# The last chunk's fourth column group: 120 rows in a load of their own, 8 rows beside the tokens, with products of their own

## The chip, the cores and the metric

The kernel runs on one core of one Trainium2 chip. The metric is the device time of one execution in microseconds, the median of several runs. The engines are TensorE (PE, with its weight loads as PEld), VectorE (DVE), ScalarE (ACT), GpSimd (POOL) and SyncE (SP). Loads and stores are issued by SP and ACT and carried out by 16 DMA engines.

## The reference

One decode step for a batch of 8 tokens, all in float32: layernorm, attention over a window of 1024 cached positions, a residual, a second layernorm, a gated MLP and a second residual.

```python
W = min(4096, max(256, Sk // 4))                 # Sk = 4096: W = 1024
q = (x @ wq) ...                                 # x: 8 x 1024, 32 heads of 128
scores = jnp.einsum("bhqd,bhkd->bhqk", q, k) * (Dh ** -0.5)   # the last W positions
p = _softmax(scores, axis=-1)
o = jnp.einsum("bhqk,bhkd->bhqd", p, v) ...  @ wo
...
g = jnp.einsum("bsd,df->bsf", x, w_gate)         # w_gate, w_up: 1024 x 3584
u = jnp.einsum("bsd,df->bsf", x, w_up)
h = _gelu(g) * u
return jnp.einsum("bsf,fd->bsd", h, w_down)      # w_down: 3584 x 1024
...
x = A_x
h = x + _A_ref(_layernorm(x, axis=-1), A_k_cache, A_v_cache, A_wq, A_wo)
h2 = h + _B_ref(_layernorm(h, axis=-1), B_w_gate, B_w_up, B_w_down)
```

## The kernel before

The weights and the caches are 111 MB and are read once. The host lays them out so that each load fills whole rows of SBUF: 128 partitions, each with one contiguous row in HBM. Two buffers, `buf[0]` and `buf[1]`, of 64 KB in each partition are filled in turn. SP issues the loads in the order of use, each with a wait for the products that last read the part of the buffer that it fills, and the queue is nearly always full.

TensorE runs one loop of seven passes: pass 0 is the query projection, 1 the scores, 2 the values, 3 the output projection, 4 (`GU0`) and 5 (`GU1`) gate and up, 6 (`DN`) down. In a pass, `products(0)` works on buffer 0 (gate, in passes 4 and 5) and `products(1)` on buffer 1 (up). A product has 32 columns of weights (8 tokens, 4 times), so it fills one of four column groups of the array, and four products that write partitions 0-31, 32-63, 64-95 and 96-127 of PSUM run beside each other. A float32 product is two matmuls in the trace. Ahead of each step TensorE waits for the semaphore `go`. GpSimd gives it: for each step it waits for all that the step needs and then counts `go` up. `turn` transposes activations (eight transposes of 128 x 128). Repeated products of no use (`repeat_residual`, L470) stand in two places of the loop.

The 3584 features of the MLP are 28 chunks of 128. `at` holds them transposed, 32 columns for a chunk. The down projection takes most chunks in the loop (pass 6, loads `wd0` to `wd2`, with 5, 2 and 1 of the 8 steps). Chunks 24 to 26 come after the loop in three loads of 128 rows by 4 KB, `ws0` to `ws2`. The last chunk, 27 (`LAST`), is cut by columns into four groups of 256 (`QW`), one for each column group, and loaded in two halves, `we0` and `we1`, with 128 of the 256 columns of each group (`ENDS`); a row of such a half is 2 KB.

After the loop TensorE does, in this order: the products of `ws0` (L534, into `ob[0]`), of `ws1` (L527, into `fin`), the fold of the sums of the loop, `d1` (L527, with `add2`), the products of `ws2` (L527), of `we0` and of `we1` (L551, into `ob[1]`). VectorE makes `d1` (L412, L415). ScalarE copies `fin` to `s_sb` (L417) once the products of `ws2` are done. VectorE adds `ob[1]` to it, one half after `we0` and one after `we1` (L421), and the two halves of the result are stored, `out0` from SP and `out1` from ACT.

The tokens `x` (8 rows of 4 KB) are loaded at the start from ACT's queue into partitions 0, 8, ..., 56 of `x_sb`, which GpSimd clears ahead of that (L177); every other partition of `x_sb` stays zero.

## Time and profile before

| | us |
|---|---|
| median of 3 runs | 264.74 (264.09 to 265.97) |
| the profiled execution: time | 264.55 |
| its span in the trace | 263.1 |
| PE busy | 149.2 |
| ACT busy | 31.1 |
| DVE busy | 26.8 |
| q1 (SP's loads), share of 16 DMA engines over the span | 98.4% |

The difference between time and span, 1.45 us, lies around the execution and is not in the trace. Busy time of an engine is a sum over the span; what sets the end is read from the chain of work that ended last.

### The profile page before, as it was taken

How to read it: one execution, taken by the hardware profiler on the slowest of the kernel's cores; microseconds unless marked ns; L12 is line 12 of the kernel's file. 1: busy time of each engine (PE TensorE's matmuls, PEld its weight loads, DVE VectorE, ACT ScalarE, POOL GpSimd, SP SyncE). 2: the span in 40 equal slices, each digit the busy share in tenths (PEclk: the TensorE clock that was granted, in tenths of full speed). 3: DMA queues.
4: the chain of work that ended last, by engine and by line, in shares of the span. 5: the costliest groups of instructions: out<-in, count | busy, mean ns of one | idle time of the engine just before them, and what ended most of it. 6: DMA issues, size and time to landing. Idle time of an engine off the chain costs nothing. (4 is left out here: it accounts for less than half of the span.)

```text
span 263.1 us, 2355 instructions
## 1 busy us (share of the span) xinstructions
PE 149.2 (57%) x1012; PEld 49.4 (19%) x1012; DVE 26.8 (10%) x45; ACT 31.1 (12%) x51; POOL 5.8 (2%) x12
## 2 busy tenths in 40 slices
PE   0024915916716717727518708817909509997985
PEld 0021211211111112122102202203302202322221
DVE  0400000000100100310500100250000200102011
ACT  1030110130020020010010000043200200201100
POOL 8000000000000000000000000000000000000000
PEclk9999985895975975956965965975976956999999
DMA  7999997999799799979979997999899999999995
GB/s 299 423 418 458 478 478 319 478 478 468 329 478 478 329 468 478 468 329 478 478 339 458 478 468 329 478 478 448 349 404 468 404 473 404 443 467 405 396 408 214
DMA packets 3617, 111.32 MB, mean 423 GB/s; under 512 B 408, under 2 KB 664, under 8 KB 1312
## 3 DMA queue, kind: packets, MB, share of 16 engines
q1 hardware_dynamic: 3456, 111.22, 98.4%
q10 hardware_dynamic: 160, 0.10, 0.1%
q14 instruction: 1, 0.01, 0.0%
HBM read 111.18 MB, written 0.13 MB: 423 GB/s over the span
## 5 line engine op out<-in xcount | busy, mean ns | idle before, releaser
L484 PE MATMUL o<-w,st 128*32 128x512 f32 x832 | 115.8, 716 | 73.7 <-PEq L457 66.9
L484 PEld LDWEIGHTS o<-w,st 128*32 128x32 f32 x832 | 32.0, 129 | 149.9 <-issue 149.9
L464 PE MATMUL tt<-ident,zeros 128*128 128x128 f32 x104 | 16.5, 311 | 35.1 <-PEq L457 35.1
L464 PEld LDWEIGHTS tt<-ident,zeros 128*128 128x128 f32 x104 | 13.3, 159 | 45.5 <-issue 45.5
L470 PE MATMUL fin<-zeros,spread 128*32 128x512 f32 x24 | 10.6, 593 | 0.0
L330 ACT COPY st<-tt 128x512 f32<-128x512 f32 x4 | 2.1, 588 | 36.2 <-PE tt L464 36.2
L320 DVE SCALAR_TENSOR_TENSOR av<-o,rtot,own 128x512 f32<-128x512 f32 x4 | 3.0, 752 | 31.3 <-PE o L484 31.3
L305 ACT ACTIVATE zeros<-o,nmax 128x1024 f32<-128x1024 f32 x2 | 2.2, 1113 | 31.9 <-DVE nmax L303 31.9
L303 DVE TENSOR_REDUCE nmax<-o 128x1 f32<-128x1024 f32 x2 | 2.4, 1224 | 34.7 <-PE o L484 34.7
L345 DVE TENSOR_TENSOR y_sb<-o,y_sb 128x512 f32<-128x512 f32 x3 | 2.1, 690 | 35.8 <-PE o L484 35.8
L285 DVE SCALAR_TENSOR_TENSOR zeros<-o,tq 128x512 f32<-128x512 f32 x2 | 1.4, 690 | 38.1 <-PE o L484 38.1
L379 DVE TENSOR_TENSOR g<-o,g 128x512 f32<-128x512 f32 x2 | 1.4, 691 | 30.6 <-PE o L484 30.6
L388 DVE TENSOR_TENSOR u<-o,u 128x512 f32<-128x512 f32 x2 | 1.4, 692 | 28.4 <-PE o L484 28.4
L284 ACT ACTIVATE tq<-o 128x512 f32<-128x512 f32 x2 | 1.2, 597 | 24.9 <-PE o L484 24.9
L470 PEld LDWEIGHTS fin<-zeros,spread 128*32 128x32 f32 x24 | 2.6, 110 | 7.2 <-issue 7.2
L352 ACT COPY zeros<-fin 32x512 f32<-32x512 f32 x1 | 0.6, 574 | 28.1 <-PE fin L515 28.1
L323 DVE TENSOR_REDUCE zeros<-av 128x128 f32<-128x1024 f32 x2 | 3.7, 1872 | 0.1
L214 POOL MEMSET zeros<- 128x3712 f32 x1 | 3.2, 3191 | 0.0
L378 ACT COPY g<-o 128x512 f32<-128x512 f32 x2 | 1.2, 585 | 16.8 <-PE o L484 16.8
L268 ACT COPY st<-tt 128x1024 f32<-128x1024 f32 x2 | 2.0, 1012 | 7.6 <-PE tt L464 7.6
L252 ACT ACT_TABLE_LOAD x2 | 2.6, 1283 | 2.9 <-POOL ident L211 2.9
L387 ACT COPY u<-o 128x512 f32<-128x512 f32 x2 | 1.2, 585 | 13.6 <-PE o L484 13.6
(58 smaller groups left out, 41.2 us busy)
## 6 DMA issues: line engine op xcount, KB each, us to landing
w<-ends SPq DMA_DIRECT2D x4, 4096.0 KB, 23.4
w<-w SPq DMA_DIRECT2D x1, 7168.0 KB, 21.8
w<-ends SPq DMA_DIRECT2D x1, 5120.0 KB, 21.6
w<-ends SPq DMA_DIRECT2D x1, 2048.0 KB, 26.1
w<-ends SPq DMA_DIRECT2D x3, 512.0 KB, 17.8
w<-w SPq DMA_DIRECT2D x1, 1024.0 KB, 4.9
w<-ends SPq DMA_DIRECT2D x1, 1024.0 KB, 28.1
w<-ends SPq DMA_DIRECT2D x2, 256.0 KB, 18.9
```

The source lines that it names most:

```text
L214: clear = run("gpsimd", lambda e: e.memset(zeros, 0.0))
L252: tok = run("scalar", lambda e: e.activation(sd, ve, AF.Sqrt), tok)
L268: a = run("scalar", lambda e: e.copy(st[0].rearrange("p (c r b) -> p c r b", c=NC, b=B), xt.unsqueeze(2).to_broadcast([P, NC, P // B, B])) ...
L303: tok = run("vector", lambda e: e.tensor_reduce(out=nmax, in_=ob[s], axis=AX.X, op=ALU.max, negate=True), pe(f"{h}1"))
L305: tok = run("scalar", lambda e: e.activation(xs[s], ob[s], AF.Exp, bias=nmax, accum_out=tot), tok)
L320: tok = run("vector", lambda e: e.scalar_tensor_tensor(av[:, i], o3, rtot, own.unsqueeze(2).to_broadcast([P, HB, DH]), op0=ALU.mult, op1=A ...
L323: tok = run("vector", lambda e: e.tensor_reduce(out=out, in_=av.rearrange("p i b d -> p d (i b)"), axis=AX.X, op=ALU.add), tok)
L330: tok = run("scalar", lambda e: e.copy(heads[:, g], turned.unsqueeze(2).to_broadcast([P, REP, P // 2 // B, B])), pe(f"t{h}2"))
L345: tok = run("vector", lambda e: e.tensor_add(y_sb, part, y_sb), ready, tok)
L464: ins = nc.tensor.transpose(t8[:, i, :], src[:, i * P:(i + 1) * P], ident)
L470: nc.tensor.matmul(fin[0:32, 0:N], spread.rearrange("p r b -> p (r b)"), h_sb[:, 0:N], start=True, stop=True)
L484: ins = nc.tensor.matmul(ob[s][32 * r:32 * r + 32, c:c + N], st[s][:, i * P + 32 * r:i * P + 32 * r + 32], buf[s][:, (i * NQ + r) * N:(i * ...
```

## The change

Of the last chunk's fourth column group (128 rows by 256 columns, 1 KB a row), the first 120 rows (`FEW`) are loaded by a load of their own, `w4`, into 120 partitions. The other 8 rows are appended to the tokens: each of the 8 rows of `x` becomes 5 KB, and `xw` takes the place of `x_sb`. `we0` and `we1` lose that group, so that their rows are 1.5 KB, and their products go from four to three each.

The fourth group is then two products into partitions 96-127 of `fin` (`ROW3` on), ahead of those of `ws0`: `at_odd` by `w_odd` (the 8 rows, on the 64 partitions of `xw`), and the first 120 partitions of `at` for chunk 27 by `w4`. The first of them starts the sum there, so the products of `ws1` no longer start it in that group. `at_odd` holds the 8 features of the 8 rows in partitions 0, 8, ..., 56. For that GpSimd clears 64 columns of `xs[1]` and writes the product of `ge` and `u1` for the last 8 features to every eighth of them; the transposes of pass 5 turn them with the rest, and ScalarE copies them out. The step of those transposes (`tb5`) waits for GpSimd's product too.

At the end ScalarE copies `fin` to `o_fin` itself, and VectorE adds into 96 of its partitions in place. The count of `gate` moves from ACT to SP.

```diff
+FEW = P - P // 16
+ROW3 = 32 * (NQ - 1)
...
-    x_sb = sb("x_sb", ROWS, D)
-    x_zero = run("gpsimd", lambda e: e.memset(x_sb, 0.0))
+    xw = sb("xw", ROWS, D + QW)
+    x_sb, w_odd = xw[:, 0:D], xw[:, D:]
+    x_zero = run("gpsimd", lambda e: e.memset(xw, 0.0))
...
-    x_in = move("x", x_sb[0:ROWS:STEP, :], x, x_zero, engine="scalar")
+    x_in = move("x", xw[0:ROWS:STEP, :], x, x_zero, engine="scalar")
...
+    t = buf[1][0:FEW, SINGLE * D:SINGLE * D + QW]
+    fourth = t, move("w4", t, fourth, pe(f"b{GU1}"))
     singles = []
...
-        a = SINGLE * D + NQ * c0
-        t = buf[1][:, a:a + NQ * n]
+        a = SINGLE * D + QW + (NQ - 1) * c0
+        t = buf[1][:, a:a + (NQ - 1) * n]
...
             late_ok = widen(STEPS // 2, STEPS, at_ok)
+            h0 = 32 * (nb - 1)
+            at_odd = sb("at_odd", ROWS, 32)
+            at_ok = run("scalar", lambda e: e.copy(at_odd, t8[0:ROWS, NC // 2, h0:h0 + 32]), pe(f"tb{k}"))
...
-    s_sb = sb("s_sb", P, QW)
-    sum_ok = run("scalar", lambda e: e.copy(s_sb, fin[:, 0:QW]), (fl.own["tensor"], len(names) + 2))
     o_fin = sb("o_fin", P, QW)
+    sum_ok = run("scalar", lambda e: e.copy(o_fin, fin[:, 0:QW]), (fl.own["tensor"], len(names) + 2))
     cut = ENDS[0]
-    halves = [(ob[1][:, 0:cut], 0, cut), (ob[1][:, N:N + QW - cut], cut, QW)]
-    done = [run("vector", lambda e: e.tensor_add(o_fin[:, a:b], d_ps, s_sb[:, a:b]),
+    halves = [(ob[1][0:ROW3, 0:cut], 0, cut), (ob[1][0:ROW3, N:N + QW - cut], cut, QW)]
+    done = [run("vector", lambda e: e.tensor_add(o_fin[0:ROW3, a:b], d_ps, o_fin[0:ROW3, a:b]),
...
-    nc.scalar.sem_inc(gate, 1)
     nc.vector.wait_ge(gate, 1).then_inc(gate, -1)
-    nc.sync.wait_ge(issued, 1)
+    nc.sync.wait_ge(issued, 1).then_inc(gate, 1)
...
+    odd = xs[1][:, N:N + ROWS]
     for name in [n for kind, n in order if kind == "wait"]:
+        if name == f"tb{GU1}":
+            release()
+            tok = run("gpsimd", lambda e: e.memset(odd, 0.0), pe(f"tb{GU0}"))
+            need[name].append(run("gpsimd", lambda e: e.tensor_mul(
+                odd.rearrange("p (i r) -> p i r", r=STEP)[:, :, 0], ge[:, N - B:N], u1[:, N - B:N]),
+                tok, b, ge_ok))
...
-                fin[32 * j:32 * j + 32, 0:QW], lhs(j), rhs(j), start=start, stop=stop),
+                fin[32 * j:32 * j + 32, 0:QW], lhs(j), rhs(j), start=start and j < NQ - 1, stop=stop),
...
+    t, here = fourth
+    for lhs, rhs, waits in ((at_odd, w_odd, (at_ok,)), (at[0:FEW, LAST, :], t, (here,))):
+        run("tensor", lambda e: e.matmul(
+            fin[ROW3:P, 0:QW], lhs, rhs, start=(lhs is at_odd), stop=False), *waits, mark=False)
...
-        for j in range(NQ):
+        for j in range(NQ - 1):
             run("tensor", lambda e: e.matmul(
                 d_ps[32 * j:32 * j + 32, :], at[:, LAST, :], t[:, j * n:(j + 1) * n],
-                start=True, stop=True), here, *o_free[1], mark=(j == NQ - 1))
+                start=True, stop=True), here, *o_free[1], mark=(j == NQ - 2))
...
+    parts += [row[0:FEW, NQ - 1]]
     parts += [down[:, i] for i in range(LAST - SINGLE, LAST)]
-    parts += [row[:, :, a:b] for a, b in zip(cuts, cuts[1:])]
+    parts += [row[:, 0:NQ - 1, a:b] for a, b in zip(cuts, cuts[1:])]
...
-        "x": np.ascontiguousarray(A_x).reshape(B, D),
+        "x": np.concatenate([A_x.reshape(B, D), row[FEW:, NQ - 1]], axis=1),
```

On TensorE after the loop, before the change (names: `o` is PSUM that the loop's products use, `w` a weight buffer, `at` the features, `d,add` the fold):

```order
L534 MATMUL o<-w,at 32x512 [waits ws0_done,scalar_done]
L534 MATMUL o<-w,at 32x512
L527 MATMUL fin<-w,at 32x256 [waits ws1_done]
L527 MATMUL fin<-w,at 32x256 x3
L527 MATMUL fin<-d,add 32x256 [waits vector_done]
L527 MATMUL fin<-d,add 32x256 x3
L527 MATMUL fin<-w,at 32x256 [waits ws2_done]
L527 MATMUL fin<-w,at 32x256 x3
```

In the same place, with the change:

```order
L551 MATMUL fin<-xw,at_odd 32x256 [waits scalar_done]
L551 MATMUL fin<-w,at 32x256 [waits w4_done]
L556 MATMUL o<-w,at 32x512 [waits ws0_done]
L556 MATMUL o<-w,at 32x512
L545 MATMUL fin<-w,at 32x256 [waits ws1_done]
L545 MATMUL fin<-w,at 32x256 x3
L545 MATMUL fin<-d,add 32x256 [waits vector_done]
L545 MATMUL fin<-d,add 32x256 x3
```

Two products stand ahead of those of `ws0`, the second behind a wait for `w4`; the rest keeps its order.

On SP, the last loads, before the change (a size is partitions by float32 elements; the loads of 1024 are `ws0` to `ws2`, those of 512 `we0` and `we1`):

```order
L107 DMA w<-ends 128x4096
L107 DMA w<-ends 128x2048
L107 DMA w<-ends 128x1024 [waits tensor_done]
L107 DMA w<-ends 128x1024 x2
L107 DMA w<-ends 128x512 x2
L107 DMA out<-o_fin 128x128 [waits vector_done]
```

The same, with the change:

```order
L109 DMA w<-ends 128x4096
L109 DMA w<-ends 128x2048
L109 DMA w<-ends 120x256 [waits tensor_done]
L109 DMA w<-ends 128x1024 x3
L109 DMA w<-ends 128x384 x2
L109 DMA out<-o_fin 128x128 [waits vector_done]
```

`w4` stands ahead of `ws0` and takes over its wait, and the two last loads are a quarter smaller.

## Rows read from the trace of the kernel before

**Rows 1.** The page: span, and the DMA engines' busy tenths in 40 slices

```profile
span 263.1 us, 2355 instructions
...
DMA  7999997999799799979979997999899999999995
```

**Rows 2.** The page's DMA queues: packets, MB, share of 16 engines

```profile
q1 hardware_dynamic: 3456, 111.22, 98.4%
```

**Rows 3.** The chain that ended last: start us, us, what

```profile
241.62 19.00 DMA w<-ends
```

**Rows 4.** The timeline of the tail, from the loop's last step

```profile
255.65 1.07 PE L484 MATMUL o<-w,st 128*32 128x512 f32 x8 [0.56 <-PEq L457]
256.89 1.05 PE L534 MATMUL o<-w,at 128*32 128x512 f32 x4 [0.18 <-DMA w<-ends]
258.05 0.69 DVE L415 TENSOR_TENSOR d<-o,d 128x512 f32<-128x512 f32 x1 [5.34 <-PE o L534]
258.08 0.64 PE L527 MATMUL fin<-w,at 128*32 128x256 f32 x8
258.79 0.64 PE L527 MATMUL fin<-d,add 128*32 128x256 f32 x8
259.35 0.64 PE L527 MATMUL fin<-w,at 128*32 128x256 f32 x8
260.04 0.43 PE L551 MATMUL o<-w,at 128*32 128x128 f32 x8
260.06 0.37 ACT L417 COPY s_sb<-fin 128x256 f32<-128x256 f32 x1 [15.67 <-PE fin L527]
260.60 0.29 DVE L421 TENSOR_TENSOR o_fin<-o,s_sb 128x128 f32<-128x128 f32 x1 [1.86 <-PE o L551]
260.67 0.43 PE L551 MATMUL o<-w,at 128*32 128x128 f32 x8 [0.20 <-DMA w<-ends]
...
261.16 0.29 DVE L421 TENSOR_TENSOR o_fin<-o,s_sb 128x128 f32<-128x128 f32 x1 [0.26 <-PE o L551]
```

**Rows 5.** Stretches of 0.1 us: the last columns are clock, DMA share, GB/s

```profile
259.70:259.80 0.10, 0.10 (x8) 0.00 (x0) 0.00 (x0) 0.00 (x0) 0.00 (x0) 1.00 0.28 82
259.80:259.90 0.10, 0.10 (x4) 0.00 (x0) 0.00 (x0) 0.00 (x0) 0.00 (x0) 1.00 0.07 21
259.90:260.00 0.10, 0.09 (x4) 0.00 (x0) 0.00 (x0) 0.00 (x0) 0.00 (x0) 1.00 0.05 20
260.00:260.10 0.10, 0.06 (x4) 0.06 (x8) 0.00 (x0) 0.04 (x1) 0.00 (x0) 1.00 0.11 41
```

**Rows 6.** The queues in the stretch 0 to 20 us: packets, MB, share

```profile
q10 hardware_dynamic: 16, 0.03, 0.4%
```

**Rows 7.** TensorE and VectorE around the end of pass 5, by the timeline

```profile
240.63 0.69 DVE L390 TENSOR_TENSOR zeros<-ge,u 128x512 f32<-128x512 f32 x1
...
241.52 1.06 PE L464 MATMUL tt<-ident,zeros 128*128 128x128 f32 x8 [1.74 <-PEq L457]
242.51 5.34 PE L470 MATMUL fin<-zeros,spread 128*32 128x512 f32 x12
248.25 4.50 PE L484 MATMUL o<-w,st 128*32 128x512 f32 x40 [0.40 <-PEq L457]
```

**Rows 8.** The start, by the timeline

```profile
0.73 0.94 POOL L177 MEMSET x_sb<- 64x1024 f32 x1 [0.29 <-POOLq L598]
...
5.46 0.23 POOL L221 TENSOR_TENSOR zeros<-ident 128x16 f32<-128x16 f32 x1
...
9.98 1.28 DVE L245 BATCH_NORM_STATS2 ln_bn<-x_sb 64x6 f32<-64x512 f32 x2 [4.34 <-DMA x_sb<-x]
...
15.72 1.01 ACT L268 COPY st<-tt 128x1024 f32<-128x1024 f32 x1 [3.81 <-PE tt L464]
...
23.20 3.64 PE L484 MATMUL o<-w,st 128*32 128x512 f32 x16 [7.51 <-PEq L457]
```

**Rows 9.** The DMA issues of the last 27 us: KB each, us to landing

```profile
out<-o_fin SPq DMA_DIRECT2D x1, 64.0 KB, 1.6
```

## The prediction

> **What bounds the kernel now.** I read the page first, then the chain that ended last, then the tail in order of time, and last the DMA engines in slices of 0.1 us. The page says that the kernel is a transfer with work beside it: the loads keep the 16 DMA engines busy for 98.4% of the span [rows 2], in nearly every slice [rows 1]. The chain ends in the same way: the stretch from 241.62 on for 19.00 us, to 260.62, is a wait for the last load [rows 3]. So only two things can move the end: when the last byte lands, and what is done behind it.

> Behind it stands little: TensorE starts the last four products at 260.67, VectorE the last addition at 261.16, 0.49 later [rows 4]. One more chain ends close to that: the products of `ws2` at 259.35, ScalarE's copy at 260.06 for 0.37, VectorE's first addition at 260.60 for 0.29, to 260.89 [rows 4]. The second addition can't start ahead of that, so at most 0.27 us (261.16 less 260.89) can be had in the tail while this chain stays where it is.

> The slices show how the transfer ends [rows 5]. One engine of 16 is a share of 0.06. From 259.80 on the share is 0.07, 0.05 and 0.11, with 21, 20 and 41 GB/s; times 0.1 us that is 2.1, 2.0 and 4.1 KB, together 8.2 KB, or four rows of 2 KB. In the slice ahead of that the share is still 0.28. So most engines are done by about 259.8, and one carries on alone for four rows, to about 260.18; 0.49 us later TensorE starts.

> **The change part by part.** Which engine carries which row. 3456 packets are 24 loads and stores of SP's queue times 144, that is 128 rows and 16 more [rows 2]; the tokens' load shows 16 packets for 8 rows [rows 6]. I read that as one packet a row and one completion for each engine that takes part: 16 engines with 8 rows each for 128 rows, 8 engines for 8 rows. No row shows a load of 120 rows. On 15 engines it would again be 8 rows each, and one engine would get nothing of it. [...]

> If the one left out is the late one, it loses 8 rows of 1 KB. An engine's 32 KB of a 512 KB load take 1.27 us (259.35 less 258.08 [rows 4]), 0.040 us a KB, so 8 KB are 0.32 us. It then ends at about 259.86, beside the next engine, which ends at about 259.88 today (the share of 0.07 is one engine and a little [rows 5]). The others keep their bytes, 32 KB in 24 rows in place of 16. Loads of 2 KB rows come at 0.63 us (260.67 less 260.04), half of 1.27, so halving a row costs nothing that shows [rows 4]. Bounds for rows of 1 and 1.5 KB: 0, and 8 more rows at the full price of a 2 KB row, 8 x 0.079 = 0.63 us. I take 0.07, near the lower end, since from 4 to 2 KB no fixed part is seen. Eight engines carry 1 KB more with the tokens, 0.04 us. The last byte is then in at 259.88 + 0.11 = 259.99, 0.19 earlier, and the second addition could start at 260.97.

> The two new products. They write one column group, so they run behind each other. The repeated products, also of one column group, take 5.34 us for 12 matmuls of 512 columns, 0.445 each [rows 7]; a matmul of 256 columns is then 0.22, and four of them 0.89 us. The loop's last step starts at 255.65; of 4.50 for 40 matmuls and 1.07 for 8 [rows 4, 7] a matmul adds 0.107 when four groups work, so the groups are free at 255.65 + 8 x 0.107 = 256.51, and the new products end at 257.40. `w4` is in by then: it adds 0.32 us to the loop's last load, in at about 255.6. The products of `ws0` start at 256.89 today [rows 4]. They use other column groups, so from below they wait only until the last of the four matmuls has started, 256.51 + 0.67 = 257.18: 0.29 late. From above they wait for a new pair that begins when the loop's last result is out (256.72) and ends with the 0.21 us that an end takes (1.07 less 0.86): 257.82, 0.93 late. I take 0.29, because four groups work beside each other in every row of the loop.

> What hangs on that: `d1` (258.05), the fold (258.79, so 259.08) and the products of `ws2`. The fold's two passes take 2 x 0.22, so these start at about 259.53 in place of 259.35, where the load held them. That moves ScalarE's copy to 260.24 to 260.61. VectorE started its first addition 0.17 after the copy's end, but may have been held by TensorE (260.04 + 0.49 = 260.53); with a handover of 0 to 0.17 it starts at 260.61 to 260.78 and ends at 260.90 to 261.07. The second addition then starts at about 261.0, after the later of this and 260.97: **0.16 us earlier**.

> What costs nothing, with its cover. GpSimd's clear at the start is a quarter longer, 0.24 us (0.94 x 1280/1024), and delays the issue of the tokens' load by as much. Layernorm starts at 9.98, ScalarE is done with the first activations at 16.73, and TensorE starts at 23.20, when the weights are in [rows 8]: 6.5 us of cover. GpSimd's product for 8 features costs about 0.23 (16 columns took that [rows 8]) beside VectorE's 0.69 at 240.63 [rows 7]; even if one waits for the other, the transposes at 241.52 come 0.23 later, and after the repeated products, which end at 247.85, 0.40 us are free until 248.25 [rows 7]. ScalarE's small copy stands ahead of one that VectorE needs at 252. SP issues one load more while the queue is 19 us ahead [rows 3]. Three products in place of four in the last halves save nothing, since four groups work at once, and an addition on 96 partitions goes over the same 128 columns.

> **The sum.** The profiled execution took 264.55 us with a span of 263.1, and 264.74 is the median of the runs; I apply the difference to the median: 264.74 - 0.16 = 264.58, so 264.6. A measurement of this kernel can tell about 1% (2.6 us) from no change.

> **The rivals.** (a) The late engine is not the one left out, or another one is late in each execution. Then it keeps its bytes in smaller rows, +0.07, and the tail ends 0.07 later: 264.8. For it: no view names the engine. [...]

> (b) Slower: the new products hold TensorE's queue. It decides from the point where `ws0`'s products start more than 0.5 us late. At the upper bound of 0.93 the fold comes at 259.72, `ws2`'s products at 260.17, the copy ends at 261.25, and the additions start at 261.3 and 261.6: 0.45 late, 265.2. Against it stands that groups overlap in the loop.

> (c) A small load of its own costs its whole way. The 64 KB of a store took 1.6 us from issue to landing [rows 9]; if `w4` put that between two loads, the time would be 264.74 + 1.6 - 0.3 = 266.0. Against it: the two last loads, 256 KB each, come 0.63 apart. [...]

> (d) The change doesn't do what it says: 120 rows don't go to 15 engines. On 8 they are 15 rows each, 7 more, +0.28 with the gain gone, 265.0; on a single engine 120 KB take 4.8 us, 4.5 more than today's share, 269.2. The tokens' 8 packets speak against both.

> **How the numbers follow.** Forecast 264.6: 0.52. (a) 264.8: 0.25. (b) 265.2: 0.12. (c) 266.0: 0.04. (d) 0.04, half of it at 265.0. Something that no row shows: 0.03. The range takes in the forecast with the largest gain (0.27 in the tail), (a), (b), the upper bound of the row cost (0.63 less 0.19, so 265.2) and how far single runs lie from their median (0.65 below, 1.23 above): 263.9 to 265.6. All but (d) on one engine lies within 1%: same 0.95, slower 0.03, faster 0.02.

> **What would show it.** In the profile after: 3591 packets on q1 if `w4` uses 15 engines (24 x 144 + 120 + 15), 3584 with 8; no engine alone for 0.3 us in the slices ahead of the end; the last products starting about 0.2 us earlier; `ws0`'s products at about 257.2; the first addition no earlier than today, and the second close behind it. The prediction is wrong if the tail is held by the new products for over 0.5 us, if the landing of the loop's loads moves, or if another engine is late.

## The result and the profile after

The changed kernel takes 265.28 us (median of 22 runs, 264.92 to 267.31), against 264.53 of the kernel before (22 runs beside it, 263.98 to 265.97). The ratio is 1.0035, with an interval of 1.0022 to 1.0047. The forecast was a gain of 0.16 us; what came is a loss of about 0.8, inside the predicted range and far below the 1% that the prediction said a measurement can tell, but with the other sign.

Each run also has its own span. Their median is 263.75 us after, and 262.8 to 262.9 before (100 runs, beside the three sets of experiments); the time outside the span stays at a median of 1.3 to 1.4. So the loss lies within the span. The median span turned out to be the sharper measure of the two, since a few long executions pull at every time; the experiments are read by both.

The page of the profiled execution after (265.6 us), its span and its DMA queues with packets, MB and share; the first two lines answer to [rows 1, 2]:

```profile
span 264.3 us, 2359 instructions
...
q1 hardware_dynamic: 3591, 111.21, 98.1%
...
q14 instruction: 3, 0.02, 0.0%
q8 instruction: 1, 0.02, 0.0%
```

3591 packets are the number that the prediction gave for `w4` on 15 engines. The two last lines are loads of instructions, not of data. Before has a single one on q14 and none on q8, but only the load on q8 and one of the three on q14 are new: the other two start at 263.65 and 263.88, at the very end, as the two of before do (263.07, and 263.27 just behind the span). The queues in the stretch 259.3 to 260.3 us of after show where the new one on q14 lies:

```profile
q1 hardware_dynamic: 232, 0.31, 86.5%
q14 instruction: 1, 0.01, 2.2%
```

It is a load of 8 KB that starts at 259.88, some 4 us behind the last step that GpSimd releases (255.76), and it takes a share of 2.2% of 16 engines in 1 us, which is 0.35 us of one engine, in the last us of the data. The chain that ended last, after (start us, us, what), answers to [rows 3]:

```profile
242.03 19.30 DMA w<-ends
261.33 0.04 issue
261.37 0.45 PE o L573 x6
261.83 0.02 issue
261.85 0.29 DVE o_fin L428
```

The form is the same, the wait for the last load ends 0.71 later (261.33 against 260.62). The tail by the timeline, after, answers to [rows 4]:

```profile
253.10 1.92 PE L502 MATMUL o<-w,st 128*32 128x512 f32 x16 [0.41 <-PEq L475]
255.76 1.06 PE L502 MATMUL o<-w,st 128*32 128x512 f32 x8 [0.74 <-PEq L475]
256.76 0.62 PE L551 MATMUL fin<-xw,at_odd 64*32 64x256 f32 x2
...
257.31 0.62 PE L556 MATMUL o<-w,at 128*32 128x512 f32 x2
...
258.54 0.64 PE L545 MATMUL fin<-w,at 128*32 128x256 f32 x8 [0.18 <-DMA w<-ends]
259.23 0.64 PE L545 MATMUL fin<-d,add 128*32 128x256 f32 x8
259.84 0.64 PE L545 MATMUL fin<-w,at 128*32 128x256 f32 x8
...
260.55 0.37 ACT L425 COPY o_fin<-fin 128x256 f32<-128x256 f32 x1 [16.05 <-PE fin L545]
260.95 0.29 DVE L428 TENSOR_TENSOR o_fin<-o,o_fin 96x128 f32<-96x128 f32 x1 [1.78 <-ACT o_fin L425]
...
261.37 0.42 PE L573 MATMUL o<-w,at 128*32 128x128 f32 x6 [0.60 <-DMA w<-ends]
261.85 0.29 DVE L428 TENSOR_TENSOR o_fin<-o,o_fin 96x128 f32<-96x128 f32 x1 [0.61 <-PE o L573]
```

Two things are to be seen. The products of `ws1` start at 258.54, 0.46 later than before, and wait for their load; from there everything stands later. And the last products have been waiting for 0.60 us when they start, where before it was 0.20: VectorE is done with the first addition at 261.24 and idles for 0.61. The second addition is 0.69 later than before.

The DMA engines in stretches of 0.1 us, after (the last columns are clock, DMA share, GB/s), answer to [rows 5]:

```profile
260.10:260.20 0.10, 0.10 (x8) 0.00 (x0) 0.00 (x0) 0.00 (x0) 0.00 (x0) 1.00 0.48 154
260.20:260.30 0.10, 0.10 (x8) 0.00 (x0) 0.00 (x0) 0.00 (x0) 0.00 (x0) 1.00 0.13 31
260.30:260.40 0.10, 0.10 (x7) 0.04 (x6) 0.00 (x0) 0.00 (x0) 0.00 (x0) 1.00 0.07 16
260.40:260.50 0.10, 0.10 (x9) 0.10 (x6) 0.00 (x0) 0.00 (x0) 0.00 (x0) 1.00 0.11 15
260.50:260.60 0.10, 0.10 (x6) 0.01 (x1) 0.00 (x0) 0.05 (x1) 0.00 (x0) 1.00 0.11 15
260.60:260.70 0.10, 0.10 (x6) 0.00 (x0) 0.00 (x0) 0.10 (x1) 0.00 (x0) 1.00 0.00 0
260.70:260.80 0.10, 0.08 (x3) 0.00 (x0) 0.00 (x0) 0.10 (x1) 0.00 (x0) 1.00 0.10 15
```

There is again one engine alone, and for longer than before: four rows of 1.5 KB start from 260.3 on (15 GB/s for 0.1 us is one row), and in the trace they take 0.11, 0.17, 0.18 and 0.15 us, where the rows ahead of them take about 0.07. The trace also has the times at which the 16 engines report that they are done with a load. For the last load of after, fifteen do so from 260.42 to 260.80 and the last at 261.33, 0.53 later; for the load ahead of it the last two engines are within 0.01. The stores, by the issues (KB each, median us to landing), answer to [rows 9], where one took 1.6:

```profile
out<-o_fin SPq DMA_DIRECT2D x1, 64.0 KB, 2.8
out<-o_fin ACTq DMA_DIRECT2D x1, 64.0 KB, 2.1
```

The load on q8 (16 KB) runs beside them, from 262.07, and one engine is done with each store late: 1.26 us behind the others with the first, 0.53 with the second. It comes in some executions only, as the experiments show.

### The profile page after: what moved, and what is told of

It reads as the page before. It is cut to its first block, busy times and chain, and to the rows that moved or that the text cites. A ratio compares the mean times of both kernels' runs of the same rounds, so it can differ in the third digit from the quotient of the medians.

```text
span 264.3 us, 2359 instructions
## 1 busy us (share of the span) xinstructions
PE 149.4 (57%) x1012; PEld 49.9 (19%) x1012; DVE 26.8 (10%) x45; ACT 31.2 (12%) x52; POOL 6.9 (3%) x14
## 3 DMA queue, kind: packets, MB, share of 16 engines
q1 hardware_dynamic: 3591, 111.21, 98.1%
## 5 line engine op out<-in xcount | busy, mean ns | idle before, releaser
L482 PE MATMUL tt<-ident,zeros 128*128 128x128 f32 x104 | 17.4, 322 | 35.2 <-PEq L475 35.2
L482 PEld LDWEIGHTS tt<-ident,zeros 128*128 128x128 f32 x104 | 14.0, 166 | 45.6 <-issue 45.6
```

The lines of the kernel that those rows point to most:

```text
L482: ins = nc.tensor.transpose(t8[:, i, :], src[:, i * P:(i + 1) * P], ident)
```

## The experiments

The theory at the outset (F in the expectations): the change lengthens an engine's instruction stream, and that brings a load of instructions which runs on one of the DMA engines of the last rows and makes it late. One rival is that the new `w4`, which fills 120 partitions and not 128, holds up the loads around it; a second, that the new products and the additions hold the tail. The expectations call the first P once it is narrowed to GpSimd's stream, the rival R, and D the case that the split load itself is the loss. The first four kernels ask which engine's stream it is. Of the next four, one adds to GpSimd's stream without the change, and three undo GpSimd's part and the 120 rows, alone and together. The last four undo the 8 rows apart, change the number of rows, run the kernel before once more, and leave out GpSimd's new clear alone.

| kernel | edit against | time, us | ratio (interval) | median span, us | 8 KB load in the tail |
|---|---|---|---|---|---|
| e1_pe_layout | after | 265.23 | 1.0033 (1.0020 to 1.0045) | 263.8 | yes |
| e2_before_pe3 | before | 264.35 | 1.0014 (0.9997 to 1.0032) | 262.8 | no |
| e3_gate_back | after | 265.20 | 1.0034 (1.0016 to 1.0053) | 263.7 | yes |
| e4_before_sp2 | before | 264.38 | 0.9997 (0.9983 to 1.0012) | 262.9 | no |
| f1_before_pool3 | before | 265.06 | 1.0016 (0.9998 to 1.0034) | 263.4 | yes |
| f2_pool_short | after | 264.70 | 1.0010 (0.9994 to 1.0025) | 263.25 | no |
| f3_w4_128 | after | 264.96 | 1.0028 (1.0011 to 1.0045) | 263.4 | yes |
| f4_both | after | 265.06 | 1.0020 (1.0004 to 1.0035) | 263.4 | no |
| g1_no_odd | after | 264.25 | 0.9996 (0.9986 to 1.0005) | 262.9 | no |
| g2_w4_112 | after | 264.51 | 1.0007 (0.9998 to 1.0015) | 263.0 | no |
| g3_before_again | before | 264.33 | 1.0001 (0.9993 to 1.0010) | 262.9 | no |
| g4_no_clear | after | 265.63 | 1.0050 (1.0030 to 1.0071) | 264.2 | no |

The ratio is to the kernel before on the same chip (264.20 for e, 264.41 for f, 264.36 for g; median spans 262.8, 262.9, 262.9).

**e1_pe_layout.** TensorE's part of F: its branch is put back to where it stands in before, by one register instruction more and the branch one product earlier.

```
-    nc.regs_mov(turns, 1)
+    nc.regs_mov(turns, 0)
+    nc.regs_alu(turns, turns, 1, op=ALU.add)
...
+            if (i, j) == (0, 2):
+                nc.tensor.br_lt(turns, PASSES + 2, on_true="last", on_false="same")
```

> The changed kernel with the same work; only TensorE's instruction stream is laid out so that its one branch stands where it stood before (one register instruction more at the start, and the branch ahead of the last of the three products of we0). Theory F (the instruction loads of the profile after, 8 KB and 16 KB that run on the loads' DMA engines near the end, come from where the instruction streams are cut into pieces; TensorE's is the one of 8 KB at 259.9 us): that load goes, the last bytes land some 0.5 us earlier and the time is about 264.8. Theory D (the split load itself is the loss: smaller rows, 15 engines): the time stays at 265.3 and the 8 KB load, if it goes, changes nothing.

It behaves as after does: 263.8, with the 8 KB load in its place. TensorE's stream isn't the cause.

**e2_before_pe3.** The other way round: before with waits that make TensorE's stream as much longer as the change does.

```
+    for i in range(7):
+        nc.tensor.wait_ge(*landed[1 + i // 2, i % 2][0])
```

> The kernel before, with three more waiting instructions on TensorE after the loop (for loads that landed long ago), so that its branch stands at the place that it has in the changed kernel. Theory F: an instruction load of 8 KB appears in the last 4 us of the loads, and the time grows by about 0.5 us, to 265.0. Theory D: no load, or one without effect, and 264.5 to 264.6.

The seven waits are three instructions more in the trace (2358 against 2355). Nothing comes of it; there is no load of instructions in the tail and the span is that of before.

**e3_gate_back.** After, with the count of `gate` given by ScalarE again, as before, so that SP has one instruction fewer.

```
+    nc.scalar.sem_inc(gate, 1)
...
-    nc.sync.wait_ge(issued, 1).then_inc(gate, 1)
+    nc.sync.wait_ge(issued, 1)
```

> The changed kernel with the count of gate moved back from SP to ACT, so SP has one instruction less after the store. Theory F with SP as the engine of the 16 KB load at 262.1 us: that load goes or comes later, the stores land after 1.6 us again in place of 2.1 to 2.8, and the time is about 264.8. If the load belongs to another engine, it stays and the time is 265.3. Theory D: 265.3.

263.7, and both loads are still there, the 8 KB at 259.93 and the 16 KB at 263.52. In this profile one engine is done with the second store 1.81 us behind the others. So this instruction of SP brings neither. **e4_before_sp2** is its counterpart: before with a wait more on SP and `gate` counted there.

```
+    for _ in range(2):
+        nc.sync.wait_ge(*pe(f"b{GU1}"))
...
-    nc.scalar.sem_inc(gate, 1)
...
-    nc.sync.wait_ge(issued, 1)
+    nc.sync.wait_ge(issued, 1).then_inc(gate, 1)
```

> The kernel before, with one more waiting instruction on SP ahead of the store (for a step that is long done) and the count of gate moved from ACT to SP, so that SP's stream has the length that it has in the changed kernel. Theory F with SP as the engine of the 16 KB load: the load appears near 262 us and the time grows by 0.3 to 0.5 us, to about 264.9. Theory D, or another engine: 264.5.

262.9, and neither load. So SP's stream falls out too, and of the engines whose order the change touches GpSimd is next: it got a clear, a product and a wait.

**f1_before_pool3.** Before, with three clears of one column each at GpSimd's start. They touch no data of the kernel and end at 6.06 us (5.89 and 0.17 by f1's timeline); layernorm starts at 9.98 in before [rows 8].

```
+    spare = sb("spare", P, 3)
+    for i in range(3):
+        nc.gpsimd.memset(spare[:, i:i + 1], 0.0)
```

> The kernel before with three small clears more on GpSimd at the start, so that its instruction stream is as long as in the changed kernel (the three write a tile that nobody reads). Theory P (the 8 KB instruction load at 259.9 us belongs to GpSimd, whose stream has grown by three instructions): the load appears about 4.3 us after GpSimd's last release (near 259.6), it hits one engine, the last load lands some 0.5 us later and the time is about 264.7 to 265.0 where before has 264.2 to 264.5. Theory D (the split load is the loss): no change, 264.3.

The 8 KB load appears. The queues of f1 in the stretch 259.3 to 260.3:

```profile
q1 hardware_dynamic: 60, 0.09, 26.3%
q14 instruction: 1, 0.01, 2.1%
```

and the end of its tail by the timeline:

```profile
260.22 0.29 DVE L424 TENSOR_TENSOR o_fin<-o,s_sb 128x128 f32<-128x128 f32 x1 [1.86 <-PE o L554]
...
260.80 0.42 PE L554 MATMUL o<-w,at 128*32 128x128 f32 x8 [0.71 <-DMA w<-ends]
261.29 0.29 DVE L424 TENSOR_TENSOR o_fin<-o,s_sb 128x128 f32<-128x128 f32 x1 [0.78 <-PE o L554]
```

The same rows of before, run once more as g3, which has no such load:

```profile
260.26 0.29 DVE L421 TENSOR_TENSOR o_fin<-o,s_sb 128x128 f32<-128x128 f32 x1 [1.87 <-PE o L551]
260.32 0.43 PE L551 MATMUL o<-w,at 128*32 128x128 f32 x8 [0.20 <-DMA w<-ends]
...
260.81 0.29 DVE L421 TENSOR_TENSOR o_fin<-o,s_sb 128x128 f32<-128x128 f32 x1 [0.26 <-PE o L551]
```

The first addition stands at the same place in both (260.22, 260.26), the last products are 0.48 later in f1, held by the DMA. With the last load fifteen engines are done from 259.95 to 260.24 in f1 and the last at 260.75; in g3 all 16 from 259.82 to 260.27. The same holds throughout: in the five profiles with the 8 KB load in the tail (after, e1, e3, f1, f3) the last engine is 0.44 to 0.56 us behind the fifteenth with the last load, and at most 0.07 with the one ahead of it; in the nine without, it is 0.01 to 0.27 behind. The end follows: in the 11 profiles in which no load on q8 meets the stores, the span ends 2.43 to 2.47 us behind the last engine's report. The median span is 0.5 longer (263.4 against 262.9; the shortest of f1's 11 spans is 263.2, and 27 of the 35 of before beside it are shorter than that). The ratio of the times, 1.0016, has an interval that just takes in 1: by the times alone this would not be told.

**f2_pool_short.** After, with the product for 8 features on VectorE and without the clear, so that GpSimd's stream is as long as in before. VectorE's gets one instruction longer.

```
+        if k == GU1:
+            odd = xs[1][:, N:N + ROWS]
+            hm_ok = run("vector", lambda e: e.tensor_mul(..., ge[:, N - B:N], u1[:, N - B:N]), hm_ok)
...
-            tok = run("gpsimd", lambda e: e.memset(odd, 0.0), pe(f"tb{GU0}"))
-            need[name].append(run("gpsimd", lambda e: e.tensor_mul(...), tok, b, ge_ok))
```

> The changed kernel with GpSimd's stream at its length of before: the product of the 8 features is made by VectorE, and the clear ahead of it is left out (the other partitions are multiplied by zeros). Theory P: no instruction load of 8 KB at 259.9, no engine alone at the end, and a time about 0.5 us under the changed kernel's, 264.6 to 264.8; what is left over before is the price of the split load. Theory D: the time stays at 265.2.

The load in the tail is gone, and the second addition follows close behind the first, as the prediction had it:

```profile
261.14 0.62 DVE L432 TENSOR_TENSOR o_fin<-o,o_fin 96x128 f32<-96x128 f32 x2 [1.73 <-ACT o_fin L429]
```

The median span falls by 0.5, to 263.25. It is still 0.35 above before.

**f3_w4_128.** After, with GpSimd as it is, and `w4` loaded for all 128 rows; the product still reads 120 of them.

```
-    t = buf[1][0:FEW, SINGLE * D:SINGLE * D + QW]
+    t = buf[1][:, SINGLE * D:SINGLE * D + QW]
...
-    parts += [row[0:FEW, NQ - 1]]
+    parts += [row[:, NQ - 1]]
```

> The changed kernel with w4 loading all 128 rows (8 KB more; the products still use 120 of them), so that 16 engines take part. Theory R (a load of 120 rows on 15 engines disturbs the loads around it: in the three profiles with it the median engine needs 0.17 to 0.36 us more from the loop's second last load to ws0 than 8 KB should cost): w4 and ws0 come 0.2 us earlier in spite of 8 KB more, and the time is 0.1 to 0.2 us under the changed kernel's, 265.1. If rows of 1 KB are what costs: no change, or 0.05 us more.

The load of instructions is there, with what it does to the last products; the steps ahead come closer together than in after:

```profile
252.86 1.92 PE L502 MATMUL o<-w,st 128*32 128x512 f32 x16 [0.40 <-PEq L475]
255.41 1.06 PE L502 MATMUL o<-w,st 128*32 128x512 f32 x8 [0.62 <-PEq L475]
...
258.16 0.64 PE L545 MATMUL fin<-w,at 128*32 128x256 f32 x8 [0.16 <-DMA w<-ends]
...
261.05 0.42 PE L573 MATMUL o<-w,at 128*32 128x128 f32 x6 [0.63 <-DMA w<-ends]
```

From the step at 252.86 to the products of `ws1` it is 5.30 us, in after 5.44 (253.10 to 258.54). Span 263.4: 0.35 less than after, 0.5 above before.

**f4_both.** The edits of f2 and f3 together.

> The changed kernel with both: GpSimd's stream at its length of before, and w4 with 128 rows on 16 engines. Theories P and R together: 264.3 to 264.5, no worse than before by more than 0.2 us. With P alone as f2; with D alone 265.2.

The profiled execution has the tail as expected:

```profile
260.70 0.63 DVE L432 TENSOR_TENSOR o_fin<-o,o_fin 96x128 f32<-96x128 f32 x2 [1.66 <-ACT o_fin L429]
```

and a span of 263.0. But the median span is 263.4, with 12 values from 262.9 to 264.4, and the time is 1.002. The additive picture (0.5 from GpSimd, 0.35 from the 120 rows) asked for 262.9; three of the 12 runs come within 0.1 of that, the others are longer by 0.4 to 1.5. This run doesn't bear the sum out. It also stands against f2: with 128 rows in place of 120 the median span should have been shorter than f2's, and it is 0.15 longer.

**g1_no_odd.** After with nothing left of the 8 rows: `w4` with 128 rows and one product for them, the tokens' load and GpSimd as in before.

```
-    x_in = move("x", xw[0:ROWS:STEP, :], x, x_zero, engine="scalar")
+    x_in = move("x", x_sb[0:ROWS:STEP, :], x, x_zero, engine="scalar")
...
-    for lhs, rhs, waits in ((at_odd, w_odd, (at_ok,)), (at[0:FEW, LAST, :], t, (here,))):
...
+        fin[ROW3:P, 0:QW], at[:, LAST, :], t, start=True, stop=False), here, at_ok, mark=False)
```

> One part of the change alone: the fourth group is loaded by itself, all 128 rows on 16 engines, and multiplied in one product; the 8 rows beside the tokens with their product, VectorE's or GpSimd's work for them and the longer rows of x are left out, so that GpSimd's stream has its length of before. Theories P and R together (instruction load of GpSimd 0.5 us, 15 engines 0.2 us): neither loss, 264.2 to 264.4, the same as before. If splitting the load or three products in place of four cost something by themselves: 264.7 or more.

The time and span are those of before: 0.9996, 262.9. The tail of g1:

```profile
252.98 1.92 PE L491 MATMUL o<-w,st 128*32 128x512 f32 x16 [0.43 <-PEq L464]
...
258.27 0.64 PE L534 MATMUL fin<-w,at 128*32 128x256 f32 x8 [0.23 <-DMA w<-ends]
...
259.56 0.64 PE L534 MATMUL fin<-w,at 128*32 128x256 f32 x8
...
260.67 0.64 DVE L424 TENSOR_TENSOR o_fin<-o,o_fin 96x128 f32<-96x128 f32 x2 [1.82 <-ACT o_fin L421]
```

From the products of `ws1` to the first addition it is 2.40 us here and 2.40 in f4 (258.30 to 260.70), which has the new pair of products: the pair costs nothing. From the loop's step (252.98) to the first addition it is 7.69, in before 7.44 (253.16 to 260.60): with `w4` in the queue the chain of the first addition is 0.25 later, and the second addition follows it closely.

**g2_w4_112.** f2 with `w4` cut to 112 rows, 8 rows of the last chunk's fourth group being left out of the sum.

```
-    t = buf[1][0:FEW, SINGLE * D:SINGLE * D + QW]
+    t = buf[1][0:FEW - STEP, SINGLE * D:SINGLE * D + QW]
```

> The changed kernel with GpSimd's stream at its length of before and w4 cut to 112 rows, which 16 engines can share with 7 rows each (8 rows of the last chunk's fourth group are left out of the result). Theory R (15 engines, or another assignment of partitions to engines than that of 128 rows): if the number of engines is the cause, the median engine needs about 2.77 us from the loop's second last load to w4 (2.49 and 7 KB); if the assignment is, it needs 0.2 us more again, about 3.0. Time 264.3 to 264.6.

Its page shows 3584 packets on q1, which is 16 engines again with 7 rows each (24 x 144 + 112 + 16). The span is 263.0, 0.25 less than f2's and 0.1 above before. The expectation also set a test: from the loop's second last load to `w4` the median engine would need 2.77 us if the number of engines is the cause, and about 3.0 if it is the way in which partitions are dealt out to engines. In the trace it needs 2.99. With 128 rows it is 2.84 to 2.86 (g1, f3, f4), with 120 rows 2.99 to 3.19 (after, e1, e3, f2, g4). So 16 engines don't help a load of 112 rows: the number of engines isn't the cause by this test.

**g3_before_again.** The kernel before, unchanged, for its tail.

> The kernel before, unchanged, for a second profile of it. If one engine is late by about 0.27 us in every execution (the premise of the forecast), the DMA share at the end of the loads shows one engine alone for 0.3 us again. If that was a matter of one execution, the last engine ends within 0.1 us of the one before it, as in the two profiles of kernels with before's loads. Time within 0.1% of before.

Its slices of 0.1 us:

```profile
259.60:259.70 0.10, 0.06 (x5) 0.01 (x1) 0.00 (x0) 0.00 (x0) 0.00 (x0) 1.00 0.41 144
259.70:259.80 0.10, 0.10 (x4) 0.10 (x8) 0.00 (x0) 0.08 (x1) 0.00 (x0) 1.00 0.06 21
259.80:259.90 0.10, 0.10 (x8) 0.05 (x7) 0.00 (x0) 0.10 (x1) 0.00 (x0) 1.00 0.01 0
```

From 0.41 the share falls to that of one engine for one slice and to nothing; in [rows 5] one went on alone for three slices. The late engine that the forecast wanted to relieve isn't there. In the profile of before one engine is 0.25 to 0.27 us behind the fifteenth with each of the last 13 loads, not only at the end; in g3 it is 0.01 to 0.03, in e2 0.09 to 0.11, in e4 0.11 to 0.13. The spans of these four are 263.1, 262.7, 262.9 and 262.9. So in these four a late engine makes the span longer by about as much as it is late, but how late it is changes from one execution to the next. From the loop's last step to the last products it is 5.01 us in g3 (255.31 to 260.32) and 5.02 in [rows 4] (255.65 to 260.67): the late engine holds the load of that step as it holds the last one.

**g4_no_clear.** After without GpSimd's clear alone, which leaves its stream one instruction longer than in before.

```
-            tok = run("gpsimd", lambda e: e.memset(odd, 0.0), pe(f"tb{GU0}"))
...
-                tok, b, ge_ok))
+                pe(f"tb{GU0}"), b, ge_ok))
```

> The changed kernel without GpSimd's clear of the 64 columns (what stands in the other partitions is multiplied by zeros), so GpSimd's stream is one instruction longer than before in place of three. Theory P: the instruction load stays if one instruction is enough to pass the edge of a block (265.0 to 265.2), and goes if two or three are needed (264.6 to 264.8).

The 8 KB load is not in the profiled tail, whose execution took 264.52, but five of the seven runs took 265.55 to 266.56, and the median is the highest of all kernels. The spans of these five are spread from 263.3 to 265.2. What happens in those runs isn't seen, since the profile caught one of the two short ones. The profile fits the branch of the expectation in which one instruction isn't enough to bring the load; the times don't (264.6 to 264.8 were expected). This run speaks neither for nor against the theory.

## Why the prediction was wrong, and where it was right

**The step that failed: "What costs nothing, with its cover".** It priced GpSimd's longer clear at the start and its product at what they take as work, 0.24 and 0.23 us, and covered both; the new clear of 64 columns (0.15 us at 236.04) it left out. The work did hide: layernorm starts at 9.99, the loop at 22.89, the step behind the repeated products at 248.19, all as before or earlier. (The cover at the start is 5.4 us and not 6.5, since ScalarE makes a second copy until 17.81; nothing hangs on that.) What wasn't priced is the loading of the instructions themselves (q14 on the page of after). Three more of them on GpSimd bring a load of 8 KB into the last us of a kernel whose end is the landing of its last load; one DMA engine then ends 0.44 to 0.56 us behind the others. The load itself takes 0.34 to 0.35 us, and the late rows take longer than others (in after, 0.11 to 0.18 in place of 0.07). That the load and the late rows are on the same engine is read from these times, since the trace doesn't name the engine. That GpSimd's instructions bring it is shown from both sides: f1 adds the instructions without the change and gets the load, 0.48 in the tail and 0.5 in the median span; f2 takes them out of the change and loses the load and 0.5. TensorE's and SP's streams are excluded (e1 to e4). No rival of the prediction had it; "something that no row shows" got a chance of 0.03 and no price. In f1 the load costs the data behind it 0.48 us. Why three instructions more bring the load to this place, the runs don't show.

**The premise that failed: the one late engine.** The gain rested on [rows 5], read as a property of the kernel: one engine with 8 KB more to do than the rest. It was that of one execution. In three other profiles with the loads of before and no 8 KB load (g3, e2, e4) the last engine is 0.01 to 0.12 us behind the fifteenth at the end, where it was 0.27. So in these three there was little to relieve; the slices of one execution can't tell a regular straggler from a chance one. That the engine that `w4` leaves out is the late one, on which the sum's landing 0.19 us earlier rests, was the author's assumption. No run shows which engine it leaves out, and in f2 an engine is 0.46 behind with the loop's last load, 0.40 with `w4` itself, and still 0.24 with the last load. That is rival (a), both halves of it, with 0.07 as its price. And two of the signs that the prediction named for being wrong came: another engine was late, and the landing of the loads moved.

**The chain that the sum moved too little: the products of `ws2` and the first addition.** The prediction had `w4` delay the loop's last load by 0.32, but moved `ws2`'s products by 0.18 only, to 259.53, although it says itself that the load held them; the load stands behind `w4` too, and should have moved by the same 0.32. Counted from the loop's step ahead, `ws2`'s products came 0.39 later in g1 (6.58 against 6.19) and 0.55 later in after (6.74), and the first addition 0.25 and 0.41 later (7.69 and 7.85 against 7.44). That eats the 0.27 that the tail had to give [rows 4]: where no load of instructions comes (f2, f4, g1, g2, g4), the first addition ends just ahead of the second, in g1 by 0.07. But this chain doesn't hold the end alone. In these five the second addition also starts 0.47 to 0.48 behind the last products, as it does where VectorE waits for them (0.49 in before, 0.48 in after), and the last products start 0.04 to 0.05 behind the landing of the last load. In g1 they stand 7.57 us behind the loop's step, in before 7.51, and the second addition 8.05 and 8.00. The landing that the sum moved 0.19 earlier did not come earlier.

**The term that was mis-sized: `w4` between the loop's loads.** It was put at 0.32 us there, to be given back by the two smaller last loads. From the loop's step ahead to the products of `ws1` (TensorE's rows) it is 4.92 us in before (253.16 to 258.08) and 4.91 in g3 (252.82 to 257.73), 5.30 in f3 and 5.29 in g1 (252.98 to 258.27), both with 128 rows, 5.44 in after, 5.42 in e3 (253.20 to 258.62) and 5.59 in e1 (252.90 to 258.49), with 120. So 128 rows cost 0.38, close to the forecast, and are given back (g1's span is before's); 120 rows cost 0.50 to 0.68, and the difference of 0.12 to 0.30 stays. The engines' own times say the same, in all 14 profiles. From the loop's second last load to the last load the median engine needs 7.64 to 7.67 us with the loads of before (before, g3, e2, e4, f1), 7.73 to 7.75 with 128 rows (g1, f3, f4), 7.87 with 112 (g2) and 7.88 to 8.08 with 120 (after, e1, e3, f2, g4). So the split costs 0.1 with 128 rows and 0.2 to 0.4 with 120.

By the median spans it is 0.35 between after and f3, which differ in the 120 rows alone. The other such pair, f2 and f4, doesn't show it (263.25 and 263.4), because most runs of f4 are long; f4's profiled execution, with 263.0, is a short one. The 120 rows were chosen to leave an engine out, and this is their price. What exactly is held up was not shown: g2's load of 112 rows has 16 engines and is held up too, so leaving out an engine is not the whole reason; that the partitions are dealt out in another way than with 128 rows is what is left of the two causes that its expectation named.

**The sum as measured.** 0.5 for the load of instructions and 0.35 for the 120 rows make 0.85; the median span grew by 0.85 to 0.95. f3 fits, with the load of instructions and 128 rows: its median is f1's, 263.4. Against the sum stands f4, which should have had neither and came out 0.5 above before in its median, and g4. Both differ from before in more than these two. In the profiles of after, e3, f1, f4 and g2 a second load of instructions, 16 KB on q8, falls on the stores or behind the kernel's end; these five executions took 265.6, 266.89, 265.94, 265.08 and 265.58 us; the eight other profiles of the changed kernel and the experiments have no such load and took 264.06 to 264.96. In after, e3 and g2 it falls on the stores, and one engine is done with a store 0.53 to 1.81 us behind the others, where it is 0.01 to 0.04 without it. It would explain a scatter of 1 to 2 us that isn't in every run, and so the long runs of f4 and g4, but that isn't shown: no run of f4 or g4 with a long span has a profile. Which engine it belongs to, and what decides in which runs it comes, stays open.

**What held.** The 15 engines and 3591 packets; in after, fifteen engines report the end of `w4` from 255.60 to 256.01, and the sixteenth count comes at 240.3, when the load is issued. No price for rows of 1 and 1.5 KB by themselves (g1 has both, and before's time). `ws0`'s products start at 257.31, forecast 257.18; in after their load lands at 257.22, so the pair is not what holds them alone. Nothing follows from it: rival (b) did not come, and the pair costs nothing (f4 against g1). Rival (c), a load of its own at its full price of 1.6 us, and (d) did not come either.

**Does the split bring anything?** g1 is the change without the 8 rows apart, and runs like before; no version here beats the kernel before.

## What to carry to other kernels

Where a kernel ends on its last transfer, look for the instruction queues in the last window of the profile (here a load of 8 KB stands there in five profiles, and in them the last engine is 0.44 to 0.56 us behind the fifteenth), and price an edit also by the instructions it adds to each engine, idle engines too. A straggler seen in one execution's slices is to be seen in a second one before a change is built on it. Loads that fill all 128 partitions are the ones whose price the neighbouring rows tell; here the median engine needed 0.13 to 0.35 us more for the last loads with 120 rows than with the same load padded to 128.

## What the runs showed of the hardware that was not expected

GpSimd's product on 8 columns took 0.71 us where 16 columns took 0.23 at the start [rows 8]. In after, VectorE's multiply of 128x512, this product and what stands behind them on TensorE, by the timeline:

```profile
240.57 0.69 DVE L395 TENSOR_TENSOR zeros<-ge,u 128x512 f32<-128x512 f32 x1
240.62 0.71 POOL L462 TENSOR_TENSOR zeros<-ge,u 128x8 f32<-128x8 f32 x1 [4.43 <-DVE u L393]
...
241.55 1.06 PE L482 MATMUL tt<-ident,zeros 128*128 128x128 f32 x8 [1.83 <-PEq L475]
...
248.19 1.06 PE L502 MATMUL o<-w,st 128*32 128x512 f32 x8 [0.31 <-PEq L475]
```

The one ends at 241.26, the other at 241.33: the two started 0.05 us apart, and GpSimd's took as long as VectorE's. Whether the one held up the other was not shown. The 0.71 us cost nothing here: the transposes start at 241.55, 0.22 behind their end, and TensorE is still idle for 0.31 us ahead of the step at 248.19, where it was 0.40 [rows 7].
